# A fused attention and GLU layer: gate and up tiles in groups of their own, tanh and product read from the banks, ScalarE's order laid out by its own clock

## The chip, the cores and the metric

One core of one Trainium2 chip runs the whole layer in one launch. The metric is device time in microseconds (us), the median of several runs. A profiled execution of the kernel lies beside it.

Five engines work side by side, each with an instruction queue of its own, and wait for each other by semaphores: TensorE (PE in the profile; PEld are its weight loads), VectorE (DVE), ScalarE (ACT), GpSimd (POOL) and SyncE (SP), which issues most DMAs. Matmuls write into banks of the accumulator memory (PSUM), 128 partitions by 512 fp32 numbers each.

## What is computed

x has 2048 rows (tokens) of 1024 numbers. First comes attention with 32 query heads of width 32 that share one key and one value head, then a gated FFN of width 3584, each behind a layer norm and with a residual. Cut from the reference:

```
h  = x + A(layernorm(x));   h2 = h + B(layernorm(h))
A: q = x @ wq (32 heads); k = x @ wk; v = x @ wv
   p = softmax(q k^T / sqrt(32));  o = p v;  return o @ wo
B: g = x @ w_gate; u = x @ w_up
   return (sigmoid(g) * u) @ w_down
```

The sigmoid is taken as 0.5 * (1 + tanh(g/2)); the factor 0.5 is applied where the down product is added to the residual.

## The kernel before: tiles, stages and what sets the order

**Tiles.** The queries are cut into 8 chunks of 256 rows. For each chunk there are 8 head groups (four heads each, 128 numbers), and for each of these 8 score bursts: 512 bursts in all. One burst (s_burst, line 472) is 8 matmuls of two key tiles by four heads, written to two pairs of the six score banks S_ps. Each pair is turned into probabilities by one exponential on ScalarE (exps, line 494; 128x1024, so 1024 exponentials), which go to a ring of 18 tiles, Pr. The PV group of a head group (pv_group, lines 562 to 583) multiplies probabilities by V and sums them; from the tenth head group on, VectorE adds probabilities in pairs first (add_pair, lines 522 and 531), so that PE's sums of ones need fewer matmuls. Then come the output projection (wo_group), the second layer norm on VectorE and GpSimd, and a DMA transpose, which gives the chunk's FFN input in QT.

**FFN of a chunk before the change.** There are 28 tiles of 128 columns of w_gate and w_up, worked on in 14 pairs. A weight half is 256 columns (one pair) of one of the two matrices, 512 KB. gu_group (line 725 on) computes one tile: 8 matmuls of gate into columns 0 to 255 of a bank, 8 of up into columns 256 to 511 (line 734). VectorE copies the bank to a slot of gu (line 753), which frees it. After the second tile of a pair ScalarE takes the tanh in gu (line 761), and VectorE forms (1 + tanh) * up into hact (line 767). When the 14 pairs are done, four down groups of 28 matmuls follow (down_group, line 797), whose result VectorE adds to the residual (line 807).

**Banks.** Everything except the scores goes through two banks, X_ps. A group takes the one that comes free first (open_group) and holds it until its evacuation.

**Weights.** load_halves issues on SP the next half as soon as a slot is on the list half_free. During the first chunk there are four slots (wgu); parts of QT, of Pr and of kT join later, as they come out of use: 21 in the end. A half is given back after its last matmul, in the second tile of the pair. w_down is loaded once, in 14 pieces on GpSimd's queue (load_wd), which hang on score bursts 84 to 110.

**Order.** The order of every engine's instructions is laid out when the program is built. The Python code keeps a clock for each engine with assumed costs (T_EXP 0.91, T_TANH 0.53 and so on) and a time for each semaphore value (_Ctr.at). The main loop stands at PE's clock and picks what PE does next: a score burst as soon as the first exponential of the burst before it is due; else a PV group; else a projection, a gate/up or a down group, matmul by matmul, so that bursts cut into groups. A burst's two exponentials are put into ScalarE's queue at once (exps); before each, act_fill puts those tanhs whose input is due by then. VectorE's waiting work (pair sums, products, layer norms) lies on the list lo and is put into its queue by dve_fill when it is due, or by force when it is needed. The engines' queues run in this order, with semaphores for what must be waited for.

So PE runs scores, PV, projections and FFN of an earlier chunk interleaved until burst 511; behind it stands a tail of PE work without exponentials: the rest of the seventh chunk's FFN and that of the eighth.

Of the kernel before, what the change touches and what calls it, by code (L numbers as in the profile page):

```python
# [12 lines left out]
P = 128  # L13
# [4 lines left out]
class _Ctr:  # L18


    def __init__(self, sem, clk=None):
        self.sem = sem
        self.n = 0
        self.waited = {}
        self.clk = clk
        self.at = {}

    def inc(self, ins, cost=0.0, lat=0.0, k=1):
# [18 lines left out]
def when(*ticks):  # L47

    return max([0.0] + [t[0].at.get(t[1], 0.0) + 0.05 for t in ticks if t is not None])
# [25 lines left out]
def bass_sequential_preLN__grouped_kv_mqa__glu_gated_glu__prompt_kernel(  # L75
# [29 lines left out]
    RP = 18  # L105
# [9 lines left out]
    with ExitStack() as es:  # L115
# [94 lines left out]
        def _(unused):  # L210
# [172 lines left out]
            def k_group(p):  # L383
                c0 = 2 * p * P

                def evac(bank, tick):
                    act_fill(tick)
# [14 lines left out]
            def vq_group(p, qs):  # L402
# [11 lines left out]
                def evac(bank, tick):  # L414
                    act_fill(tick)
# [66 lines left out]
            def exps(k):  # L482
                for n in (2 * k, 2 * k + 1):
                    act_fill((c_s, n + 1))
                    need(act, (c_s, n + 1))
                    r = ring(k)
                    if r is None:
                        need(act, pv0_val.get(k // 2 - 3))
                    elif r >= RP // 2:
                        w = r - RP // 2 + 1  # L490
                        assert w <= pv_done[0], ("P ring", n, pv_done[0])
                        need(act, (c_pv, w), add_half.get(k - RP // 2))
                    pr = n % 3
                    c_e.inc(act.activation(out=p_tile(k, n % 2).rearrange("p (a b) -> p a b", a=2),  # L494
                                           in_=S_ps[:, 2 * pr:2 * pr + 2, :], func=ACTF.Exp, scale=SCALE), T_EXP, 0.12)

                if k // BPG >= G_SUM:
                    add_pair(k)
# [222 lines left out]
            gi = [0]  # L721
            gu_read = {}
            hact_val = {}

            def gu_group(c, ft):
                u = 2 * (c * NFP + ft // 2)
                f0 = (ft % 2) * P
                items = []
                for w in range(2):
                    for dt in range(DT):  # L730
                        def f(bank, w=w, dt=dt):
                            i = half_at[u + w]
                            need(pe, half_val[u + w])
                            ins = pe.matmul(bank[:, w * QC:(w + 1) * QC], lhsT=halves[i][:, dt, f0:f0 + P],  # L734
                                            rhs=QT[:, dt, c * QC:(c + 1) * QC], start=(dt == 0), stop=(dt == DT - 1))
                            tick = mm_done(ins, QC, dt == DT - 1)
                            if dt < DT - 1:
                                return None
                            if ft % 2 == 1:
                                half_free.append((i, [tick]))  # L740
                                if ft == NFT - 1 and w == 1 and c < NQC - 1:
# [3 lines left out]
                        items.append((QC * T_MM, f))  # L745

                def evac(bank, tick):
                    i1 = gi[0]
                    gi[0] += 1
                    r = i1 % NGU  # L750
                    force("s", lambda: i1 < NGU or i1 - NGU in gu_read)
                    need(dve, tick, gu_read.get(i1 - NGU))
                    v = c_dve.inc(dve.tensor_copy(out=gu[:, r, :], in_=bank), 0.61, 0.08)  # L753
                    if ft % 2 == 1:
                        g_ = gu[:, r - 1:r + 1, 0:QC]
                        u_ = gu[:, r - 1:r + 1, QC:2 * QC]
                        tv = [None]

                        def tanh():
                            need(act, v)  # L760
                            tv[0] = c_act.inc(act.activation(out=g_, in_=g_, func=ACTF.Tanh, scale=0.5), T_TANH, 0.1)  # L761

                        def stt():
                            while tv[0] is None:
                                act_work.popleft()[1]()
                            need(dve, tv[0], down_last[c - 1] if c else pv0_val[BPG - 1])
                            hact_val[(c, ft)] = c_dve.inc(dve.scalar_tensor_tensor(  # L767
                                out=hact[:, ft - 1:ft + 1, :], in0=g_, scalar=1.0, in1=u_, op0=ALU.add, op1=ALU.mult), 0.61, 0.08)
                            gu_read[i1 - 1] = gu_read[i1] = hact_val[(c, ft)]
                        act_work.append((v, tanh))  # L770
                        if k[0] >= NB:
                            act_work.popleft()[1]()
                        put("s", 0.61, stt, lambda: when(tv[0]) if tv[0] else None)
                    return v
                return _Group(items, evac, [hnT_val[c * TPQ], hnT_val[c * TPQ + 1]])
# [13 lines left out]
            def down_group(c, tt, dc):  # L789
                t = c * TPQ + tt  # L790
                items = []
                for ft in range(NFT):
                    def f(bank, ft=ft):
                        f1 = ft | 1
                        force("s", lambda: (c, f1) in hact_val)
# [29 lines left out]
            for c in range(NQC):  # L825
                ffn_list += [("gu", c, ft) for ft in range(NFT)]
# [21 lines left out]
            def next_group():  # L848
# [8 lines left out]
                if ffn_list:  # L857
# [4 lines left out]
                    c, u = a[1], 2 * (a[1] * NFP + a[2] // 2)  # L862
                    if c * TPQ + 1 in hnT_val and max(when(hnT_val[c * TPQ + i]) for i in range(TPQ)) <= now and u + 1 in half_val:
                        if when(half_val[u]) <= now + 0.3 and when(half_val[u + 1]) <= now + 1.0:
                            ffn_list.popleft()
                            return gu_group(c, a[2])
# [62 lines left out]
            while True:  # L929
                if q_done and not q_done[0].items and q_tick[0] is None:  # L930
                    q_tick[0] = (c_pe, c_pe.n)
                if q_tick[0] and wd_next[0] < NFP and k[0] >= WSL + WD_AT + 2 * wd_next[0]:
                    load_wd()
                kk = k[0]
                pv_ready = pv_next[0] < NQC * NQ and kk >= min(BPG * (pv_next[0] + 1) + 1, NB)
                can_s = kk < NB and pv_done[0] >= ring(kk) - RP // 2 + 1
                if can_s and k_pe[0] >= when((c_e, 2 * kk - 1)):
                    dve_fill(k_pe[0] + min([0.3] + [x.left() for x in (cur[0], pv[0]) if busy(x)]))
                    s_burst(kk)
                    exps(kk)  # L940
# [25 lines left out]
                starved = not q_list and bool(ffn_list) and ffn_list[0][0] == "gu" and ffn_list[0][1] * TPQ + 1 not in h_done  # L966
# [13 lines left out]
                if busy(cur[0]):  # L980
                    run_item(cur[0])
# [4 lines left out]
                if (pv_next[0] < NQC * NQ and kk > BPG * pv_next[0] + 1 and ffn_list and ffn_list[0][0] == "gu"  # L986
# [7 lines left out]
                if idle > 400 and act_work:  # L994
                    act_work.popleft()[1]()
                assert idle < 4000
            assert not lo
# [32 lines left out]
```

## Time and profile before

| | us |
|---|---|
| median of 3 runs | 1147.73 |
| lowest and highest | 1146.86 and 1151.37 |
| profiled execution | 1150.66 |
| its span (first to last instruction) | 1148.8 |
| PE busy / ScalarE busy / VectorE busy in the span | 1099.0 / 1012.9 / 860.0 |
| 1024 exponentials (line 494), busy | 949.0 and 15.6 |
| 112 tanhs (line 761), busy | 83.3 |
| 224 copies of banks (line 753), busy | 153.5 |
| 112 products (line 767), busy | 76.7 |

How to read it: the page's first part has each engine's busy time, the second the busy share in 40 slices of 28.7 us (9 is 90% or more). Groups are instructions of one line, with the mean of one in ns and the idle time of the engine before them. A ScalarE instruction's duration reaches over the start of the next one, so rates are read from starts, in the timeline. The chain of work goes back from the last instruction to what released it at each step; in order of time it reads as "start, duration, what". A table of windows has, for each stretch of time, the busy time of each engine and in brackets its instructions, then PE's granted clock, the DMA engines' share and their GB/s.

### The profile page before, as it was taken

The numbers are of one execution on the slowest core, as the hardware profiler recorded it, in microseconds if no ns is written. First come the engines' busy times: TensorE is split into PE (matmuls) and PEld (weight loads), VectorE is DVE, ScalarE is ACT, GpSimd is POOL, SyncE is SP. The second block draws the span as 40 slices with busy tenths as digits, with TensorE's granted clock in tenths as the row PEclk, the third lists the DMA queues.
The fourth block names the chain that finished last, engine by engine and source line by source line (L and its number), as shares of the span: only waits on it lengthen the run. The fifth ranks groups of instructions, "written<-read, shape, count | busy, mean of one in ns | idle before, by whom it ended". The sixth has DMA issues, their size and how long they took to land.

```text
span 1148.8 us, 33975 instructions
## 1 busy us (share of the span) xinstructions
PE 1099.0 (96%) x14875; PEld 667.7 (58%) x14944; DVE 860.0 (75%) x1540; ACT 1012.9 (88%) x1168; POOL 58.9 (5%) x122
## 2 busy tenths in 40 slices
PE   3799999889999999999999999999999999999998
PEld 2564446664457644775467644775467554766784
DVE  7433346877899878998889987999788987884351
ACT  5999999989999999999999999999999999970010
POOL 3200001100100001000100010001000000001000
PEclk9899999999999999999999999999999999999999
DMA  9910006964146612674146621764237551679800
GB/s 231 252 38 2 2 11 173 313 208 113 29 135 195 192 47 57 190 206 135 38 126 187 188 65 43 211 188 122 54 115 200 147 116 32 184 208 273 211 1 19
DMA packets 284180, 150.96 MB, mean 131 GB/s; under 512 B 40704, under 2 KB 278272, under 8 KB 284032
## 3 DMA queue, kind: packets, MB, share of 16 engines
q1 hardware_dynamic: 276256, 138.17, 45.9%
q0 software_dynamic: 2544, 9.44, 2.3%
q8 instruction: 117, 1.92, 0.7%
q10 hardware_dynamic: 5232, 1.18, 0.7%
q14 instruction: 31, 0.25, 0.1%
HBM read 136.18 MB, written 4.19 MB: 122 GB/s over the span
## 4 chain that ended last, share of the span: by engine, by line
PE 74%; ACT 11%; DVE 7%; issue 4%; DMA 3%; POOL 1%; DVEq 0%; ACTq 0%
PE X_ps L734 32%; PE X_ps L797 12%; PE S_ps L472 11%; ACT Pr L494 10%; PE X_ps L583 8%; PE X_ps L290 8%; DMA wgu<-in_B_w_up_dram 2%; PE X_ps L562 2%; DVE pairs L522 1%; PE X_ps L580 1%; DVE pairs L531 1%; DVE st L300 1%; ACT hact L494 1%; DVE st L678 1%; DMA zone<-hn 0%
## 5 line engine op out<-in xcount | busy, mean ns | idle before, releaser
L494 ACT ACTIVATE Pr<-S_ps 128x1024 bf16<-128x1024 f32 x1008 | 949.0, 1179 | 8.2 <-PE S_ps L472 8.1
L522 DVE TENSOR_TENSOR pairs<-Pr 128x1024 bf16<-128x1024 bf16 x432 | 290.6, 685 | 66.6 <-ACT Pr L494 61.8
L734 PE MATMUL X_ps<-QT,wgu 128*128 128x256 bf16 x2048 | 272.0, 275 | 5.9 <-DMA wgu<-in_B_w_up_dram 5.4
L734 PEld LDWEIGHTS X_ps<-QT,wgu 128*128 128x128 bf16 x2048 | 189.5, 98 | 63.9 <-issue 32.0
L797 PE MATMUL X_ps<-zone,hact 128*128 128x512 bf16 x852 | 205.6, 380 | 6.1 <-issue 4.8
L472 PE MATMUL S_ps<-QT,kT 32*128 32x256 bf16 x4096 | 204.3, 274 | 7.4 <-ACT Pr L494 4.2
L753 DVE COPY gu<-X_ps 128x512 f32<-128x512 f32 x224 | 153.5, 685 | 27.3 <-PE X_ps L734 25.2
L734 PE MATMUL X_ps<-QT 128*128 128x256 bf16 x1264 | 171.2, 273 | 0.0
L583 PE MATMUL X_ps<-Pr,V 128*32 128x256 bf16 x4032 | 162.4, 274 | 1.5 <-DVE gu L753 1.1
L761 ACT ACTIVATE gu<-gu 128x512 f32<-128x512 f32 x112 | 83.3, 744 | 85.8 <-DVE gu L753 85.8
L531 DVE TENSOR_TENSOR pairs<-pairs 128x1024 bf16<-128x1024 bf16 x216 | 148.7, 688 | 10.6
L472 PEld LDWEIGHTS S_ps<-QT,kT 32*128 32x128 bf16 x4096 | 60.8, 92 | 155.3 <-ACT Pr L494 136.2
L797 PEld LDWEIGHTS X_ps<-zone,hact 128*128 128x128 bf16 x896 | 78.6, 98 | 102.1 <-issue 22.5
L734 PEld LDWEIGHTS X_ps<-QT 128*128 128x128 bf16 x1264 | 116.8, 98 | 30.9 <-issue 18.2
L583 PEld LDWEIGHTS X_ps<-Pr,V 128*32 128x32 bf16 x4032 | 98.3, 96 | 27.8 <-issue 18.4
L290 PE MATMUL X_ps<-zone 128*128 128x256 bf16 (+2 forms) x501 | 77.2, 299 | 23.2 <-ACT hn L338 14.3
L767 DVE SCALAR_TENSOR_TENSOR hact<-gu 128x512 bf16<-128x512 f32 x112 | 76.7, 686 | 12.1 <-ACT gu L761 12.1
L601 DVE COPY ols<-X_ps 128x256 f32<-128x256 f32 x64 | 27.0, 422 | 69.0 <-PE X_ps L583 54.1
L290 PEld LDWEIGHTS X_ps<-zone 128*128 128x128 bf16 x512 | 39.4, 101 | 52.7 <-issue 14.7
L290 PE MATMUL X_ps<-wo,QT 128*128 128x512 bf16 x242 | 59.4, 380 | 1.6 <-issue 1.3
L307 POOL TENSOR_SCALAR vz<-mv 128x1 bf16<-128x1 bf16 (+1 forms) x24 | 9.1, 379 | 903.5 <-DVE mv L682 891.7
L807 DVE SCALAR_TENSOR_TENSOR hx<-X_ps,hx 128x512 bf16<-128x512 f32 x32 | 22.0, 688 | 41.9 <-PE X_ps L797 41.7
(54 smaller groups left out, 508.3 us busy)
## 6 DMA issues: line engine op xcount, KB each, us to landing
wgu<-in_B_w_gate_dram SPq DMA_DIRECT2D x72, 512.0 KB, 5.0
wgu<-in_B_w_up_dram SPq DMA_DIRECT2D x56, 512.0 KB, 5.1
QT<-in_B_w_up_dram SPq DMA_DIRECT2D x47, 512.0 KB, 5.2
QT<-in_B_w_gate_dram SPq DMA_DIRECT2D x32, 512.0 KB, 5.3
zone<-in_B_w_down_dram POOLq DMA_DIRECT2D x14, 512.0 KB, 7.0
hx<-in_A_x_dram SPq DMA_DIRECT2D x16, 256.0 KB, 2.9
out_dram<-hx SPq DMA_DIRECT2D x32, 128.0 KB, 1.7
Pr<-in_B_w_up_dram SPq DMA_DIRECT2D x8, 512.0 KB, 6.1
```

The costliest lines, as they stand in the source:

```text
L290: ins = pe.matmul(sel(bank), lhsT=a, rhs=b, start=(i == 0), stop=(i == last))
L472: ins = pe.matmul(S_ps[:, bank, kt * QC:(kt + 1) * QC], lhsT=kT4[DH * j:DH * (j + 1), (2 * b + kt) * P:(2 * b + kt + 1) * P], rhs=QT[DH * ...
L494: c_e.inc(act.activation(out=p_tile(k, n % 2).rearrange("p (a b) -> p a b", a=2), in_=S_ps[:, 2 * pr:2 * pr + 2, :], func=ACTF.Exp, scale= ...
L522: add_half[k] = slot_use[slot] = c_dve.inc(dve.tensor_tensor(out=pairs[:, slot, :].rearrange("p (j q) -> p j q", j=4), in0=p4[:, :, 0, :], ...
L531: slot_use[x] = slot_use[y] = c_dve.inc(dve.tensor_tensor(out=pairs[:, x, :], in0=pairs[:, x, :], in1=pairs[:, y, :], op=ALU.add), T_ADD, ...
L583: ins = pe.matmul(bank[DH * j:DH * (j + 1), 0:QC], lhsT=V[:, 2 * b + kt, :], rhs=rhs(j), start=first and summed, stop=last and not summed, ...
L601: dve.tensor_copy(out=ols[:, 0:QC], in_=bank[:, 0:QC])
L734: ins = pe.matmul(bank[:, w * QC:(w + 1) * QC], lhsT=halves[i][:, dt, f0:f0 + P], rhs=QT[:, dt, c * QC:(c + 1) * QC], start=(dt == 0), sto ...
L753: v = c_dve.inc(dve.tensor_copy(out=gu[:, r, :], in_=bank), 0.61, 0.08)
L761: tv[0] = c_act.inc(act.activation(out=g_, in_=g_, func=ACTF.Tanh, scale=0.5), T_TANH, 0.1)
L767: hact_val[(c, ft)] = c_dve.inc(dve.scalar_tensor_tensor(out=hact[:, ft - 1:ft + 1, :], in0=g_, scalar=1.0, in1=u_, op0=ALU.add, op1=ALU.m ...
L797: ins = pe.matmul(bank, lhsT=hact[:, ft, tt * P:(tt + 1) * P], rhs=wd[:, ft, dc * 512:(dc + 1) * 512], start=(ft == 0), stop=(ft == NFT - 1))
```

## The change

1. A group now computes both tiles of a pair for one matrix: a gate group (16 matmuls, one half) and an up group (16 matmuls, the other half) take the place of two mixed groups. A half is given back after its own group.
2. The copies are gone. ScalarE takes the tanh from the gate group's bank into a slot of gu (half as wide as before, so four pairs fit), and this frees the bank. VectorE forms the product from gu and the up group's bank, which frees that one.
3. Exponentials are no longer queued at once. A burst puts its two on exp_queue; tanhs wait on act_work with the time from which they can start; act_next picks, by ScalarE's clock, what can start first (a tanh up to 0.1 us later than an exponential goes ahead). act_run does so up to PE's clock at each step of the main loop, exp_emit when something needs an exponential that is not queued yet; exp_guess estimates its time until then.
4. open_group asks a bank that waits for a tanh for an estimated time (free). If none is free yet, the main loop lets up to 3 us pass on PE's clock, so that something else may come between.
5. A gate or an up group is picked when its own half is due within 0.3 us; before, a group asked for its gate half within 0.3 and its up half within 1.0.

The core of the diff:

```diff
@@ class _Ctr, need
+    def time(self, n):
+        if self.guess is not None and n > self.n:
+            return self.guess(n)
+        return self.at.get(n, 0.0)
...
+    for t in ticks:
+        if t is not None and t[0].emit is not None and t[1] > t[0].n:
+            t[0].emit(t[1])
@@ open_group
+            def bank_time(b):
+                f = bank_free[b]
+                return 1e9 if f == "open" else f(False) if callable(f) else when(f)
...
-                b = min((when(bank_free[b]), b) for b in range(2) if bank_free[b] != "open")[1]
+                b = min((bank_time(b), b) for b in range(2) if bank_free[b] != "open")[1]
                 g.bank = b
-                need(pe, bank_free[g.bank])
-                bank_free[g.bank] = "open"
+                f = bank_free[b]
+                need(pe, f(True) if callable(f) else f)
+                bank_free[b] = "open"
@@ ScalarE's order
-            def act_fill(*ticks):
-                while act_work and when(act_work[0][0]) < max(k_act[0], when(*ticks)) + 0.1:
+            def act_next():
+                s_e = max(k_act[0], exp_ready(exp_queue[0])) if exp_queue else 1e9
+                s_t = max(k_act[0], act_work[0][2]()) if act_work else 1e9
+                return (s_t, False) if s_t <= s_e + 0.1 else (s_e, True)
+            def act_one(is_exp):
+                if is_exp:
+                    one_exp(exp_queue.popleft())
+                else:
                     act_work.popleft()[1]()
+            def act_run(until):
+                while exp_queue or act_work:
+                    s, is_exp = act_next()
+                    if s > until:
+                        return
+                    act_one(is_exp)
+            def exp_emit(n):
+                while c_e.n < n:
+                    act_one(act_next()[1])
+            def exp_guess(n):
+                t = k_act[0]
+                for x in range(c_e.n, n):
+                    t = max(t, exp_ready(x)) + T_EXP
+                return t + 0.12
@@ the groups
-            def gu_group(c, ft):
...
-                    v = c_dve.inc(dve.tensor_copy(out=gu[:, r, :], in_=bank), 0.61, 0.08)
...
+            def half_group(c, fp, w, evac, after):
+                u = 2 * (c * NFP + fp) + w
+                items = []
+                for j in range(2):
                     for dt in range(DT):
...
+                            need(pe, half_val[u])
+                            ins = pe.matmul(bank[:, j * QC:(j + 1) * QC], lhsT=halves[i][:, dt, j * P:(j + 1) * P],
                                             rhs=QT[:, dt, c * QC:(c + 1) * QC], start=(dt == 0), stop=(dt == DT - 1))
...
+                            if j == 1 and dt == DT - 1:
                                 half_free.append((i, [tick]))
...
+            def gate_group(c, fp):
...
+                    def tanh():
+                        need(act, tick, gu_read.get(n - NGU))
+                        tanh_val[n] = c_act.inc(act.activation(out=slot, in_=bank, func=ACTF.Tanh, scale=0.5), T_TANH, 0.1)
...
+                    act_work.append((tick, tanh, lambda: when(tick, gu_read.get(n - NGU))))
+                    return free
...
+            def up_group(c, fp):
...
+                    while n not in tanh_val:
+                        act_one(act_next()[1])
+                    need(dve, tick, tanh_val[n], down_last[c - 1] if c else pv0_val[BPG - 1])
+                    hact_val[(c, 2 * fp + 1)] = gu_read[n] = c_dve.inc(dve.scalar_tensor_tensor(
+                        out=hact[:, 2 * fp:2 * fp + 2, :], in0=slot.rearrange("p (a b) -> p a b", a=2), scalar=1.0,
+                        in1=bank.rearrange("p (a b) -> p a b", a=2), op0=ALU.add, op1=ALU.mult), 0.61, 0.08)
@@ next_group, main loop
-                    if c * TPQ + 1 in hnT_val and max(when(hnT_val[c * TPQ + i]) for i in range(TPQ)) <= now and u + 1 in half_val:
-                        if when(half_val[u]) <= now + 0.3 and when(half_val[u + 1]) <= now + 1.0:
+                    if c * TPQ + 1 in hnT_val and max(when(hnT_val[c * TPQ + i]) for i in range(TPQ)) <= now and u in half_val:
+                        if when(half_val[u]) <= now + 0.3:
...
+                act_run(k_pe[0])
...
-                    exps(kk)
+                    exps(kk, now=False)
...
+                    if cur[0].bank is None and k_pe[0] + 0.02 < min(bank_time(b) for b in range(2)) < k_pe[0] + 3.0:
+                        k_pe[0] += 0.02
+                        dve_fill(k_pe[0])
+                        continue
```

More of the change, by code (lines that the diff above doesn't have):

```diff
@@ L26, in __init__ @@
         self.at = {}
+        self.guess = self.emit = None
     def inc(self, ins, cost=0.0, lat=0.0, k=1):
@@ L480, in _, with one_exp, exps @@
             pv0_val = {}
[L482 to L497, printed above, removed]
+            def one_exp(n):
+                k = n // 2
+                need(act, (c_s, n + 1))
+                r = ring(k)
+                if r is None:
+                    need(act, pv0_val.get(k // 2 - 3))
+                elif r >= RP // 2:
+                    w = r - RP // 2 + 1
+                    assert w <= pv_done[0], ("P ring", n, pv_done[0])
+                    old = k - RP // 2
+                    if old >= G_SUM * BPG:
+                        force("p", lambda: old in add_half)
+                    need(act, (c_pv, w), add_half.get(old))
+                pr = n % 3
+                c_e.inc(act.activation(out=p_tile(k, n % 2).rearrange("p (a b) -> p a b", a=2),
+                                       in_=S_ps[:, 2 * pr:2 * pr + 2, :], func=ACTF.Exp, scale=SCALE), T_EXP, 0.12)
+            def exps(k, halves=(0, 1), now=True):
+                exp_queue.extend(2 * k + i for i in halves)
+                if now:
+                    exp_emit(2 * k + halves[-1] + 1)
+                if k // BPG >= G_SUM and 1 in halves:
                     add_pair(k)
@@ L754, in evac @@
[L754 to L773, printed above, removed]
```

63 lines of the change are left out of this document (31 added, 32 removed).

## The prediction, made before the changed kernel ran

> **What bounds the kernel now.** I read the page's first three parts first.
>
> ```profile
> PE 1099.0 (96%) x14875; PEld 667.7 (58%) x14944; DVE 860.0 (75%) x1540; ACT 1012.9 (88%) x1168; POOL 58.9 (5%) x122
> ...
> ACT  5999999989999999999999999999999999970010
> ...
> DMA  9910006964146612674146621764237551679800
> ```
>
> TensorE (PE) is busy nearly all the time, and ScalarE (ACT) too, until the last exponential (about 1024 us, slice 36); only then is ScalarE free. VectorE (DVE), which the change relieves, has a quarter of the span to spare. So I ask per stage whether PE or ScalarE ends last. For that I need the price of each piece of PE work. The chain of work in order of time has them:
>
> ```profile
> 344.41 0.33 PE S_ps L472 x8
> 344.74 1.53 PE X_ps L734 x13
> ...
> 1072.99 48.91 PE X_ps L734 x448
> 1121.95 10.74 PE X_ps L797 x49
> ```
>
> In the tail 448 gate/up matmuls follow each other at 48.91/448 = 0.109 us, down matmuls at 0.219. Thirteen between two score bursts take 1.53 = 13 x 0.109 + 0.11: a change between scores, attention sums (PV) and full-array matmuls costs 0.11 us. A score burst of 8 takes 0.33, so 0.22 and one such change. Four PV matmuls of one step take 0.11. ScalarE's prices come from the timeline:
>
> ```profile
> 341.11 7.49 ACT L494 ACTIVATE Pr<-S_ps 128x1024 bf16<-128x1024 f32 x8
> ...
> 348.46 0.65 ACT L761 ACTIVATE gu<-gu 128x512 f32<-128x512 f32 x1
> 348.98 3.79 ACT L494 ACTIVATE Pr<-S_ps 128x1024 bf16<-128x1024 f32 x4
> ```
>
> Eight exponentials start over 7.35 us, and the next one starts 0.52 us after a tanh: instructions overlap by their ends, so what counts is start to start: 0.905 to 0.92 for an exponential (0.904 is the commonest), 0.52 for a tanh. A burst feeds two exponentials, 1.81 us.
>
> Now I lay both program orders side by side, eight score bursts at a time, price each engine's work by these rows and take the larger. Bursts are counted from 0 to 511; times are where the burst stands in the trace.
>
> | bursts | larger of PE and ACT, before | measured before | larger, after |
> |---|---|---|---|
> | 80 to 120 (176.8 to 265.1 us) | 79.2 | 88.3 | 80.5 |
> | 120 to 160 (to 340.1) | 74.3 | 75.0 | 73.9 |
> | 160 to 511 (to 1022.4) | 682.9 | 682.3 | 683.4 |
>
> From 340 us on, the larger of the two explains the trace to 0.1%. PE alone would need 680.5 of the 682.9: the two engines are balanced to a few tenths per cent, so relief for one alone buys almost nothing. Only bursts 80 to 120 hold real waiting, 9.1 us. The windows and the chain tell what it is:
>
> ```profile
> 205.00:210.00 5.00, 4.78 (x53) 3.41 (x51) 4.90 (x9) 4.71 (x6) 0.72 (x1) 1.00 1.10 322
> ...
> 240.00:245.00 5.00, 2.16 (x18) 1.36 (x19) 2.02 (x5) 3.09 (x5) 0.72 (x1) 0.86 1.10 320
> ```
>
> ```profile
> 201.56 6.41 DMA wgu<-in_B_w_up_dram
> ...
> 219.35 8.21 DMA wgu<-in_B_w_up_dram
> ...
> 234.13 8.66 DMA wgu<-in_B_w_up_dram
> ```
>
> The last column is GB/s, the one before it the busy share of the 16 DMA engines: saturated at about 320. There the weight halves of the first FFN chunk and w_down come in together, only four half slots exist, and PE stands up to 3 us waiting for an up half.
>
> **The change, part by part.**
>
> *VectorE.* 224 copies of 685 ns go: 153 us off VectorE. The 112 products stay; one operand now comes from a bank. Line 767 (operands in SBUF) takes 686 ns, line 807 (one operand a bank) 688, so nothing is added. VectorE's 75% lay beside PE and ScalarE, which are full: I put the gain at nothing. Nine waits of PE's PV steps for VectorE (2.1 us in all, by the spacing of PE's weight loads) bound it from above; nothing of this relief can lose.
>
> *Tanh from the bank.* No row shows a tanh that reads a bank. The nearest: four copies of 256 columns from SBUF (line 876) start 0.306 us apart; the exponential after a 256-column copy from a bank (line 389) starts after 0.264. So 0.042 less is one bound (0.478) and 0.52 the other; I take the middle, 0.50, since function and output type differ from both rows. Over the 92 tanhs among bursts 80 to 511 that is 1.8 us of ScalarE (0 to 3.9), but in the stretches with tanhs PE has 16.3 us of work per eight bursts against ScalarE's 16.0, so PE covers it: the table moves by 0.5 between the two bounds.
>
> *PE's order.* The matmuls are the same 14944. Changes between kinds fall from 1124 to 1118, 0.7 us, already in the table. But the split moves. After the last burst stood 595 gate/up matmuls, now 628: 33 x 0.109 = 3.6 us more in the tail, where nothing runs beside them. The reason shows in bursts 120 to 160: PE has 65.1 us of work there against 71.6 before, while ScalarE needs 73.9: the first chunk's FFN is used up earlier, PE runs dry, and the work missing there is paid at the end.
>
> *Banks.* A gate bank is now freed by ScalarE, behind exponentials. Of 112 tanhs, 70 stand in ScalarE's order one exponential short of all bursts issued at the gate group's end, 36 after all, 6 two short. PE's next user of that bank comes at least 1.75 us (an up group of 16) later in all but five cases. A score burst in between waits for the very exponential that the tanh follows, which ties the two queues together: priced by rows, the tanh is done 0.22 us or more before PE needs it, save twice (PV groups, 0.6 and 0.7 us). Cost: 1.3 us; none in bursts where PE's order has the slack anyway. An up bank waits for a tanh long done and 0.69 of product, less than the 1.75 of the next group. Behind a waiting product on VectorE stand the pair sums, which PV needs; with 153 us freed I cost that at nothing, and if a product waited as line 767 does now (12.1 us over 18) it would still be VectorE's idle time.
>
> *Weight halves.* This is the one gain. Before, both halves of a pair are held for 24 of its 32 matmuls; now each for 16. So the time from giving a slot back to needing it again, two pairs later, grows by 8 matmuls: about 0.9 us, with a share of the bursts 1.0. Where pairs follow closely (4.07 us), it goes from 5.1 to 6.1 us; halves take 5.5 to 8.9 us to land in this stretch. SP issues the same DMAs in nearly the same order, POOL's w_down loads hang on the same bursts. Six large waits shrink by up to 1 us each, those behind them with them. Bounds: nothing, or all 9.1. Against all of it stands bandwidth: three pairs per 16.3 us and w_down's four 0.52 MB loads are 5.2 MB, 322 GB/s, just what the windows show at best. I take 6.5 off, 2.6 us of waits left. The Trainium skill (DMA: Bandwidth & Descriptors, Specifications) gives a core about 358 GB/s from HBM; no window here passes 322. By its figure the lack would be one of latency alone, and an estimate would put all 9.1 us back, 1144.6 instead of 1147.2; rival 3 holds that case.
>
> **Sum.** +1.3 (80 to 120) - 0.4 - 0.0 + 0.5 (160 to 511) + 3.6 (tail) + 1.3 (banks) - 6.5 (halves) - 0.3 (waits for VectorE) = -0.5 us. The profiled execution took 1150.66 (span 1148.8), 2.9 above the median 1147.73 of runs from 1146.86 to 1151.37; the difference is taken off the median: **1147.2 us**, no change.
>
> **Rivals.**
> 1. *The halves give nothing* (bandwidth alone binds: the engines are at 1.1 of their share in most of the stretch). Then the tail's 3.6 and the rest stay: 1147.2 + 6.5 = 1153.7. Against: 230 to 235 us moves only 130 GB/s, so slots, not bandwidth, bound part.
> 2. *ScalarE stands at a tanh* (the slower side). A tanh now waits for PE itself, and exponentials wait behind it. By the two orders, priced by rows, ScalarE comes to a tanh 0.3 us or more after the gate group's end. It decides where PE runs over 0.3 us later against ScalarE than laid out. For it: DMA waits of 0.5 to 3 us strike PE inside groups. Against: the same bursts hold both engines together, and after 260 us the spacing of PE's weight loads shows one wait over 0.6 us. If the 92 tanhs lost 0.12 us each on average, 11 us: 1158. The Trainium skill (PSUM — Partial Sum Buffer, Engine vs sequencer instructions) calls ScalarE's queue strictly first in, first out, which is this rival's ground; here line 761 idled 85.8 us in 19 waits, nearly all after the last exponential, so its price among bursts is not shown.
> 3. *Faster*: all 9.1 us of waits go, the tanh takes 0.478 and VectorE's 2.1 us of waits vanish: 1147.2 - 2.6 - 0.5 - 1.8 = 1142.3; with the bank waits absent 1141.
> 4. *The order does not do what it says* (the planner's clock is off, so tanhs are late and banks with them): 1.3 becomes some 5, 1151.
>
> **Chances.** Forecast (1144.5 to 1150) 0.49, rival 1 0.16, rival 2 0.12, rival 3 0.15, rival 4 0.08. Half a per cent, 5.7 us, is about what a measurement of this kernel can tell: faster is below 1142.0, slower above 1153.5. Of rival 3 two thirds lie below; half of rival 1 lies above, and rival 2 whole: faster 0.10, same 0.70, slower 0.20. The range, 1141.5 to 1154, leaves out rival 2 (0.12), the upper end of rival 1 (0.05) and the lower of rival 3 (0.03).
>
> **What would show it.** Line 753 gone; tanh start to start near 0.48 to 0.52; bursts 160 to 511 again about 682 us; the stretch from burst 80 to 120 near 83 instead of 88 us with shorter DMA pieces in its chain; last exponential about 4 us earlier, and a tail 3.6 longer. I am wrong if PE waits for line 801 (tanh) by several us in total, if ScalarE's idle time before tanhs grows among the bursts, or if exponentials themselves change pace.

## The result, and the profile after

The changed kernel took 1155.29 us (median of 5 runs, 1151.48 to 1156.39), the kernel before 1148.18 in the runs beside it (1146.86 to 1151.37): a ratio of 1.0053, 95% interval 1.0034 to 1.0072. It is slower by half a per cent, where 1147.2 in 1141.5 to 1154 was forecast. The profiled execution took 1155.29, its span 1153.5, 4.7 more than the span before. That execution of before was itself 2.5 above its median, so the medians lie further apart than the spans. PE's granted clock goes with this: of the 53 runs of before beside the experiments, the twelve with a mean granted clock of 0.997 or more took 1144.83 to 1148.51 us, the eight with 0.993 or less 1149.99 to 1152.5, and the profiled execution had 0.992.

The page of the changed kernel, first and second part:

```profile
PE 1098.6 (95%) x14874; PEld 668.4 (58%) x14944; DVE 733.3 (64%) x1316; ACT 1012.3 (88%) x1168; POOL 58.5 (5%) x122
...
ACT  5999999999999999999999999999999999960110
PEclk9999999999979999999999999999999999999999
DMA  9910006992047621665146630764236550689700
```

VectorE lost 127 us of work (153 was forecast), and nothing came of it, as forecast. New is the 7 in PE's granted clock in slice 11 (317 to 346 us). Lines 472, 494, 734, 761, 797 of before are 516, 540, 782, 801, 846 here, line 583 is 633. ScalarE's timeline:

```profile
345.61 3.82 ACT L540 ACTIVATE Pr<-S_ps 128x1024 bf16<-128x1024 f32 x4
349.23 0.69 ACT L801 ACTIVATE gu<-X_ps 128x512 f32<-128x512 f32 x1
349.71 3.88 ACT L540 ACTIVATE Pr<-S_ps 128x1024 bf16<-128x1024 f32 x4
```

From the tanh's start to the next exponential's it is 0.48 us; the commonest distance of all is 0.477, the lower bound of the forecast. The chain of work in order of time, in the tail:

```profile
1021.22 0.33 PE S_ps L516 x8
1021.55 2.07 PE X_ps L782 x18
...
1037.74 15.72 PE X_ps L782 x144
1053.51 10.74 PE X_ps L846 x49
```

Prices of matmuls have not moved (15.72/144 = 0.109). But between the last output projection and the seventh chunk's down groups 144 gate/up matmuls follow each other; before there were 112 in 12.23 us. The difference is the 3.5 us by which the tail grew (32 of the 33 matmuls more that the prediction counted).

Measured as in the prediction, by where bursts stand (us). The stretches are those of the one profiled execution, whose own time stands beside the median. PE work is what the order of the program holds, by the same prices. The tail goes from burst 511 to the last weight load. Half clock is the time between 170 and 350 us in which PE's granted clock was 0.5:

| kernel | median of runs | profiled execution | bursts 80-120 | PE work there | 120-160 | PE work there | 160-511 | tail | half clock |
|---|---|---|---|---|---|---|---|---|---|
| before | 1148.18 | 1150.66 | 88.3 | 76.8 | 75.0 | 71.6 | 682.3 | 123.1 | 6.8 |
| changed | 1155.29 | 1155.29 | 86.8 | 79.7 | 77.2 | 65.1 | 682.7 | 126.6 | 13.6 |
| e1_late_pick | 1143.94 | 1144.15 | 82.7 | 77.1 | 74.8 | 72.7 | 682.1 | 122.7 | 0 |
| e2_exp_at_once | 1150.25 | 1153.72 | 88.8 | 79.3 | 76.5 | 69.7 | 682.4 | 122.7 | 10.2 |
| e3_gate_copied | 1155.11 | 1157.31 | 89.5 | 79.8 | 77.0 | 64.9 | 683.1 | 125.0 | 13.6 |
| e4_pe_kept_warm | 1151.94 | 1151.96 | 86.0 | 79.7 | 74.3 | 70.5 | 682.7 | 126.6 | 0 |
| e5_late_giveback | 1155.19 | 1155.80 | 87.9 | 79.7 | 76.4 | 65.1 | 682.7 | 126.6 | 10.2 |
| e6_before_late_pick | 1143.46 | 1143.46 | 80.9 | 72.6 | 75.3 | 74.9 | 683.3 | 121.2 | 0 |
| e7_half_wdown | 1148.69 | 1148.22 | 80.7 | 79.7 | 76.0 | 65.1 | 682.7 | 126.6 | 10.2 |
| e8_later_pick | 1142.51 | 1142.51 | 79.7 | 74.0 | 75.4 | 75.0 | 682.7 | 122.7 | 0 |
| e9_old_rules | 1140.94 | 1139.51 | 81.8 | 75.5 | 76.0 | 75.9 | 682.9 | 118.0 | 0 |
| e10_before_new_pick | 1154.03 | 1152.88 | 87.1 | 78.9 | 75.6 | 68.8 | 682.8 | 124.8 | 6.8 |

In before the 6.8 us at half clock lie in bursts 80 to 120 (178.8 to 182.2 and 243.6 to 247.0 us), in e2 and e3 3.4 of theirs (from 196 us); all others lie in bursts 120 to 160. e2's execution was 3.5 and e3's 2.2 above their medians, the slowest of their runs, so their stretches are on the long side.

From before to changed: -1.5 + 2.2 + 0.4 + 3.5 = 4.6, the 4.7 of the spans. The first two places are these. In the first stretch PE still blocks on weight halves, now at the start of gate groups (chain of work in order of time, changed kernel):

```profile
185.93 7.88 DMA wgu<-in_B_w_gate_dram
...
203.97 7.30 DMA wgu<-in_B_w_gate_dram
...
221.33 8.02 DMA wgu<-in_B_w_gate_dram
...
239.40 7.78 DMA wgu<-in_B_w_gate_dram
```

These are PE's waits for halves, of before and of the changed kernel (in all, times, longest), and the windows of bursts 80 to 120, of before and of the changed kernel (after the stretch and its length: PE, PEld, DVE, ACT, POOL busy with instructions, granted clock, DMA share, GB/s):

```profile
PE X_ps L734 <- DMA wgu<-in_B_w_up_dram: 5.4, 5, 2.9
PE X_ps L782 <- DMA wgu<-in_B_w_gate_dram: 4.8, 4, 1.5
```

```profile
176.80:265.10 88.30, 81.37 (x1105) 55.09 (x1106) 71.16 (x125) 80.69 (x94) 10.18 (x14) 0.96 0.83 241
176.80:263.60 86.80, 80.70 (x1119) 54.96 (x1120) 57.25 (x98) 81.35 (x95) 10.19 (x14) 1.00 0.89 257
```

With one wait of 0.3 us for an up half the changed kernel's waits come to 5.1 us in five, so in sum they hardly moved; they went from up halves to gate halves. What did change is the clock: 0.96 in before, for two stretches of 3.4 us at half clock, in which PE was busy throughout. At half the speed that is up to 3.4 us lost in before, and nothing in the changed kernel.

In the second stretch PE runs dry. The windows of the changed kernel, then of before:

```profile
315.00:320.00 5.00, 1.88 (x28) 0.39 (x20) 3.53 (x6) 5.00 (x6) 0.00 (x0) 0.59 0.07 23
320.00:325.00 5.00, 4.65 (x80) 2.59 (x84) 3.63 (x8) 3.76 (x5) 0.00 (x0) 0.50 0.30 57
```

```profile
315.00:320.00 5.00, 4.09 (x38) 1.36 (x36) 4.23 (x10) 5.00 (x6) 0.56 (x2) 1.00 0.40 78
320.00:325.00 5.00, 4.09 (x58) 2.50 (x59) 4.84 (x8) 5.00 (x7) 0.00 (x0) 1.00 0.24 80
```

PE is busy 1.88 of 5 us, its clock goes to one half, and in the next window ScalarE, full until then, idles 1.24 us. The timeline of the changed kernel shows how (PE, then ScalarE):

```profile
320.35 0.61 PE L516 MATMUL S_ps<-QT,kT 32*128 32x256 bf16 x8 [1.22 <-ACT Pr L540]
...
321.15 2.35 PE L633 MATMUL X_ps<-Pr,V 128*32 128x256 bf16 x40
...
323.64 0.61 PE L516 MATMUL S_ps<-QT,kT 32*128 32x256 bf16 x8
...
324.29 1.94 ACT L540 ACTIVATE Pr<-S_ps 128x1024 bf16<-128x1024 f32 x2 [1.24 <-PE S_ps L516]
```

At half clock 40 PV matmuls take 2.35 us (at full clock 40 took 1.27), the score burst behind them is late, and ScalarE waits for it. Over bursts 120 to 160 its exponentials, where they follow each other, lie 2.9 us in all further apart than 0.905 each, against 0.7 before.

### The profile page after: what moved, and what is told of

The parts are those of the page before. It is cut to its first block, busy times and chain, and to the rows that moved or that the text cites. A ratio compares the mean times of both kernels' runs of the same rounds, so it can differ in the third digit from the quotient of the medians.

```text
span 1153.5 us, 33948 instructions
## 1 busy us (share of the span) xinstructions
PE 1098.6 (95%) x14874; PEld 668.4 (58%) x14944; DVE 733.3 (64%) x1316; ACT 1012.3 (88%) x1168; POOL 58.5 (5%) x122
## 4 chain that ended last, share of the span: by engine, by line
PE 71%; ACT 14%; DVE 6%; issue 4%; DMA 3%; POOL 1%; DVEq 0%; ACTq 0%; another core or an unknown queue 0%
PE X_ps L782 31%; PE X_ps L846 13%; ACT Pr L540 12%; PE S_ps L516 11%; PE X_ps L633 8%; PE X_ps L304 6%; DMA wgu<-in_B_w_gate_dram 3%; PE X_ps L612 2%; DVE pairs L572 2%; PE X_ps L630 1%; DVE st L314 1%; DVE pairs L581 1%; ACT hact L540 1%; DVE st L728 1%; ACT gu L801 1%
## 5 line engine op out<-in xcount | busy, mean ns | idle before, releaser
L572 DVE TENSOR_TENSOR pairs<-Pr 128x1024 bf16<-128x1024 bf16 x432 | 294.4, 687 | 166.4 <-ACT Pr L540 158.3
L782 PE MATMUL X_ps<-QT,wgu 128*128 128x256 bf16 x2048 | 261.8, 274 | 5.1 <-DMA wgu<-in_B_w_gate_dram 4.8
L782 PE MATMUL X_ps<-QT 128*128 128x256 bf16 x1248 | 160.5, 273 | 0.0
L801 ACT ACTIVATE gu<-X_ps 128x512 f32<-128x512 f32 x112 | 75.8, 677 | 88.6 <-PE X_ps L782 87.7
L821 DVE SCALAR_TENSOR_TENSOR hact<-gu,X_ps 128x512 bf16<-128x512 f32 x112 | 76.3, 682 | 67.8 <-PE X_ps L782 67.1
L304 PE MATMUL X_ps<-zone 128*128 128x256 bf16 (+2 forms) x501 | 77.2, 299 | 23.4 <-ACT hn L352 14.2
L651 DVE COPY ols<-X_ps 128x256 f32<-128x256 f32 x64 | 26.9, 421 | 65.1 <-PE X_ps L633 54.2
L612 PE MATMUL X_ps<-pairs,ones 128*32 128x256 bf16 x864 | 53.5, 276 | 0.8 <-DVE pairs L581 0.7
```

Of the source, the lines that this page charges most:

```text
L304: ins = pe.matmul(sel(bank), lhsT=a, rhs=b, start=(i == 0), stop=(i == last))
L572: add_half[k] = slot_use[slot] = c_dve.inc(dve.tensor_tensor(out=pairs[:, slot, :].rearrange("p (j q) -> p j q", j=4), in0=p4[:, :, 0, :], ...
L612: ins = pe.matmul(bank[DH * j:DH * (j + 1), QC:2 * QC], lhsT=ones[:], rhs=pairs[:, HOME[b], j * QC:(j + 1) * QC], start=False, stop=b == S ...
L651: dve.tensor_copy(out=ols[:, 0:QC], in_=bank[:, 0:QC])
L782: ins = pe.matmul(bank[:, j * QC:(j + 1) * QC], lhsT=halves[i][:, dt, j * P:(j + 1) * P], rhs=QT[:, dt, c * QC:(c + 1) * QC], start=(dt == ...
L801: tanh_val[n] = c_act.inc(act.activation(out=slot, in_=bank, func=ACTF.Tanh, scale=0.5), T_TANH, 0.1)
```

## The experiments

**Theory A**, formed from this: no engine got slower. The planner starts the first chunk's pairs earlier than the halves come. So PE still blocks on halves with score bursts queued behind the blocked group; the chunk's work is used up earlier; PE runs dry in bursts 144 to 160, at half clock besides; and what could have filled it is paid in the tail. **Theory B**: bandwidth alone sets the first stretch. **Theory C**: tanh from the bank, and ScalarE's queue, cost the time. A theory D comes in with e6 alone.

**e1_late_pick** (changed kernel):

```diff
-                        if when(half_val[u]) <= now + 0.3:
+                        if when(half_val[u]) <= now + (0.3 if c else -2.0):
```

> The changed kernel, but in the first chunk a gate or up group is picked only when its half was due 2 us ago by the planner's clock (instead of 0.3 us ahead). Theory A (the planner spent the earlier refills on starting pairs earlier, so PE still blocks on weight halves in bursts 80 to 120, runs dry in bursts 144 to 160, and pays the deferred work in the tail): the larger of PE and ScalarE is 79.7 us in bursts 80 to 120, measured 80 to 83 instead of 86.8; bursts 120 to 160 take 75 instead of 77.2, no half clock at 316 us; the tail is 122 instead of 126.6 because 587 instead of 628 gate/up matmuls are left. About 1144 us, 8 to 12 below the changed kernel, at or below the kernel before. Theory B (bandwidth alone sets bursts 80 to 120): that stretch stays at 86 to 88 and only the tail's 4 us and the clock's 2 us come back, 1149. Theory C (ScalarE's queue stands at tanhs whose input comes from PE): no stage but the tail moves, 1151.

1143.94 us, ratio to before 0.996 (0.9944 to 0.9976). Every stretch went where A had put it: 82.7, 74.8, 682.1, 122.7, and no half clock. B fails as the whole story, and C.

**e2_exp_at_once** (changed kernel):

```diff
-                    exps(kk, now=False)
+                    exps(kk)
```

> The changed kernel with one part undone: a burst's two exponentials go to ScalarE's queue at once, as in the kernel before; groups, tanh and product stay. Theory A: what counts is where PE's work falls. In this order 588 gate/up matmuls are left for the tail and bursts 120 to 160 hold 69.7 us of PE work (65.1 in the changed kernel, 71.6 before), so tail 122 and those bursts 75 to 76; bursts 80 to 120 as in the changed kernel, 84 to 87. About 1148 us. Theory C: ScalarE's order by its own clock is what makes the tanh from the bank bearable; without it the waits for tanh grow in every stretch with tanhs and bursts 160 to 511 take 690 us or more instead of 682.7, 1158 or more.

1150.25, ratio 1.0018 (1.0003 to 1.0033). Tail 122.7 and 682.4 as A had it; bursts 120 to 160 took 76.5, with half clock, a little over the 75 to 76 expected; bursts 80 to 120 took 88.8 where 84 to 87 was expected, in an execution 3.5 above the median that had the half clock there too. C fails: ScalarE's new order is not what makes the tanh bearable.

**e3_gate_copied** (changed kernel, gate_group's evacuation):

```diff
+                    need(dve, tick, gu_read.get(n - NGU))
+                    v = c_dve.inc(dve.tensor_copy(out=slot, in_=bank), 0.61, 0.08)
                     def tanh():
-                        need(act, tick, gu_read.get(n - NGU))
-                        tanh_val[n] = c_act.inc(act.activation(out=slot, in_=bank, func=ACTF.Tanh, scale=0.5), T_TANH, 0.1)
+                        need(act, v)
+                        tanh_val[n] = c_act.inc(act.activation(out=slot, in_=slot, func=ACTF.Tanh, scale=0.5), T_TANH, 0.1)
...
+                    act_work.append((v, tanh, lambda: when(v)))
+                    return v
```

> The changed kernel, but VectorE copies the gate group's bank to gu (112 copies) and frees it, and the tanh is taken in gu; groups and ScalarE's order by its own clock stay. Theory A: the tanh from the bank costs and gains nothing; bursts 160 to 511 take 682 to 684, bursts 80 to 160 stay near 164, the tail is 1.7 shorter by its 614 matmuls left: 1152 to 1155 us. Theory C: ScalarE and the gate bank were the loss, 3 us or more come back among bursts 160 to 511 and 80 to 160, 1149 or less.

1155.11, ratio 1.005 (1.0034 to 1.0066): the same as the changed kernel. Bursts 160 to 511 and the tail came as A had it (683.1 and 125.0); bursts 80 to 160 took 166.5 instead of 164, in the slowest execution of the eight. Taking the tanh out of the bank gives nothing back; C falls.

**e4_pe_kept_warm** (changed kernel; warm() is called where the main loop lets PE's clock pass, and picks a free bank b):

```diff
+                if not 140 <= k[0] <= 164 or not b:
+                    return
...
+                pe.matmul(X_ps[:, b[0], 0:256], lhsT=wo[:, 0, 0:P], rhs=wo[:, 0, 0:256], start=True, stop=True)
```

> The changed kernel, with some 50 matmuls that belong to nothing (128x256, into a free bank, read by nobody) where PE would idle in bursts 140 to 164; everything else is in the same order. Theory A with the clock as its part: PE's granted clock stays at 1.0 from 310 to 335 us, bursts 120 to 160 take 74 to 74.5 instead of 77.2, everything after is earlier by as much: 2.5 us below the changed kernel. If the half clock is only seen there and costs nothing (ScalarE ends last anyway), bursts 120 to 160 stay at 77 or grow by the added work, 0 to +2 us.

1151.94, ratio 1.0031 (1.0016 to 1.0046), against 1.0053 (1.0034 to 1.0072) for the changed kernel. The intervals overlap, so what the clock cost is read from the stretch: bursts 120 to 160 took 74.3 as expected. Its windows:

```profile
315.00:320.00 5.00, 3.74 (x46) 2.02 (x47) 3.59 (x6) 5.00 (x7) 0.00 (x0) 1.00 0.01 3
320.00:325.00 5.00, 4.47 (x100) 2.51 (x100) 3.80 (x9) 5.00 (x6) 0.00 (x0) 1.00 0.31 59
```

The trace has 39 useless matmuls; with them PE's clock stays at 1.00 and ScalarE at 5.00 of 5, in the changed kernel's order of work: the half clock cost 2.9 us of the stretch. The kernels with the same order bear this out: with 0, 10.2, 10.2 and 13.6 us at half clock (e4, e7, e5, changed) the stretch takes 74.3, 76.0, 76.4 and 77.2. In the changed kernel no gap of PE between 312 us and the fall at 315.9 was longer than 0.91 us, nor any later one there longer than 1.44, and PE was busy 1.8 of the 3.4 us before the fall. The Trainium skill (TensorE: Matmul & The Clock Gate, What's actually happening) lists the half clock as the state after an idle window of about 3.4 us. The Trainium skill (TensorE: Matmul & The Clock Gate, Why this matters for your kernels) asks for no idle gaps of PE over about 3 us. Here the clock fell without any gap of that length, and the measurement decides.

**e5_late_giveback** (changed kernel, half_group; the up group gives the gate half back after its eighth matmul, and a gate group gives nothing back):

```diff
+                            if w == 1 and j == 0 and dt == DT - 1:
+                                half_free.append((half_at[u - 1], [tick]))
+                                load_halves()
+                            if w == 0:
+                                return tick
```

> The changed kernel, but a gate half is given back 8 matmuls later, after the first half of the up group, as in the kernel before; no engine's order moves (three late groups only read other slots). It measures the term that the prediction put at 6.5 us by itself. If the earlier refill is worth what was predicted (about 1 us at each of some six waits), bursts 80 to 120 go from 86.8 to 91 to 93 and the time rises by 4 to 6 us, 1159 to 1161. Theory A's other part (the waits are set by when PE asks, which lies too early by the planner's clock, and by the bandwidth both loads share): 0 to 2 us, 1155 to 1157.

1155.19, ratio 1.0063 (1.0043 to 1.0082), against 1.0053. Bursts 80 to 120: 87.9 for 86.8. PE waits for halves 5.4 us, in six waits, for 5.1. The earlier refill of the gate halves, on which PE now waits, is worth about 1 us in that stretch, and nothing that the medians show. Its chain tells why:

```profile
187.48 6.56 DMA wgu<-in_B_w_gate_dram
...
205.50 6.96 DMA wgu<-in_B_w_gate_dram
...
223.83 6.90 DMA wgu<-in_B_w_gate_dram
...
242.08 6.42 DMA wgu<-in_B_w_gate_dram
```

Asked for later, the halves take 0.3 to 1.4 us less: they wait for the DMA engines wherever they are asked. e5 speaks of the gate halves alone: the up halves, which a pair now needs 8 matmuls later than before, keep their gain in it, and no run takes that back by itself.

**e6_before_late_pick** (the kernel before, nothing of the change):

```diff
-                        if when(half_val[u]) <= now + 0.3 and when(half_val[u + 1]) <= now + 1.0:
+                        if when(half_val[u]) <= now + (0.3 if c else -0.5) and when(half_val[u + 1]) <= now + (1.0 if c else 0.2):
```

> The kernel before with nothing of the change, but in its first chunk a group is picked only when its gate half was due 0.5 us ago and its up half is due within 0.2 us (before: due within 0.3 and 1.0). Theory A: the late pick, not the groups, is what the better version lives on. PE and ScalarE give 78.4, 75.1 and 683.3 for bursts 80 to 120, 120 to 160, 160 to 511, and 582 instead of 595 gate/up matmuls are left for a tail of 121.5; with 3 to 4 us of waits left in the first stretch that is about 1143 us. Theory D (the late pick helps only with gate and up groups of their own, since only these refill early): bursts 80 to 120 stay at 86 to 88, 1148.

1143.46, ratio 0.9956 (0.9933 to 0.998); bursts 80 to 120 took 80.9. The late pick serves the kernel before as well; D fails.

**e7_half_wdown** (changed kernel; half of w_down is left out of the computation):

```diff
-                wd_val[0] = dma(pool, wd[:, f0:f0 + 2, :],
+                wd_val[0] = dma(pool, wd[:, f0:f0 + 1, :],
...
-                                        rhs=wd[:, ft, dc * 512:(dc + 1) * 512], start=(ft == 0), stop=(ft == NFT - 1))
+                                        rhs=wd[:, ft & ~1, dc * 512:(dc + 1) * 512], start=(ft == 0), stop=(ft == NFT - 1))
```

> The changed kernel, but each of the 14 w_down loads brings only its first half, 0.26 MB, and the down matmuls read that half twice: half of w_down is left out of the computation. No engine's order moves. Theory B (in the first chunk the halves wait for bandwidth that w_down's loads take): bursts 80 to 120 fall from 86.8 to 81 to 82 and the time by 5, 1150; bursts 120 to 160 stay at 77 and the tail at 126.6, since PE's order is the same. If the waits are the refill's own time only, with bandwidth to spare: 85 to 87, 1154 to 1155.

1148.69, ratio 1.0004 (0.9987 to 1.0021): 6.6 below the changed kernel. Bursts 80 to 120 fall to 80.7 with PE's order unchanged, and no wait of PE for a half is left; the other stretches move by 1.2 or less. So B is right about where the waits come from: w_down's loads. With e8 it is half of the truth: there the same bytes leave no wait either, since PE asks late.

**e8_later_pick**: as e1, with -3.0 in place of -2.0.

> As e1_late_pick, but a half must have been due 3 us ago instead of 2. The same 587 gate/up matmuls are left for the tail. Theory A: PE asks later still, so the 3 us of waits that e1_late_pick kept in bursts 80 to 120 (82.7 against 79.7) shrink to 1 or 2, the larger of PE and ScalarE there is 78.9, bursts 120 to 160 75.2 and the rest 683.8: 1142 to 1144 us. If the margin only trades waits for PE idling elsewhere, no difference from 1143.9.

1142.51, ratio 0.9956 (0.994 to 0.9972). Bursts 80 to 120 took 79.7, less even than expected, though PE has only 74.0 us of work there. No wait of PE for a DMA is left: PE idles between groups and no longer inside them, score bursts go ahead, and ScalarE is busy for all of the 79.7 us. One 5 us window moved 335 GB/s, for 322 at most before. The Trainium skill (DMA: Bandwidth & Descriptors, Specifications) gives a core about 358 GB/s from HBM. No window here reaches that.

**e9_old_rules** (changed kernel; e5's edit, and):

```diff
-                        if when(half_val[u]) <= now + 0.3:
+                        if when(half_val[u]) <= now + 0.3 and (a[0] == "u" or u + 1 in half_val and when(half_val[u + 1]) <= now + 1.0):
```

> The changed kernel with the two old rules on weight halves together: the gate half is given back 8 matmuls later (as in e5_late_giveback), and a gate group is picked only when its up half is in the queue and due within 1.0 us. Groups of one matrix, tanh and product from the banks and ScalarE's order by its own clock all stay. Here PE's order does move: 75.5 us of PE work in bursts 80 to 120, 75.9 in 120 to 160 (65.1 in the changed kernel), 551 gate/up matmuls left for the tail. Theory A: the loss comes from the planner's two rules on halves alone, not from anything that an engine does. Larger of both 79.4 plus 1 to 2 us of waits, 75.9, 683.6, tail 118: about 1140 us, the best of all. Theory C (tanh and banks cost ScalarE or PE time): some of it remains, 1147 or more.

1140.94, ratio 0.9939 (0.9917 to 0.9961), the fastest version, with all else of the change in place. Its bursts 80 to 120 stand at 175.6 to 257.4 us and 120 to 160 at 257.4 to 333.4. Two windows that cover most of them:

```profile
176.80:256.00 79.20, 74.68 (x1075) 51.62 (x1068) 55.79 (x96) 77.56 (x91) 10.21 (x14) 1.00 0.90 261
256.00:332.00 76.00, 75.96 (x1006) 39.37 (x1005) 59.14 (x106) 76.00 (x86) 4.06 (x8) 1.00 0.34 90
```

PE is busy 75.96 of 76 us where it ran dry in the changed kernel. Each rule alone leaves PE's order as in the changed kernel: e5 has the give-back alone, and with the pick alone the code lays out the very program of the changed kernel. Only both together spread the first chunk.

**e10_before_new_pick** (the kernel before):

```diff
-                        if when(half_val[u]) <= now + 0.3 and when(half_val[u + 1]) <= now + 1.0:
+                        if when(half_val[u]) <= now + 0.3 and when(half_val[u + 1]) <= now + 3.0:
```

> The kernel before with one condition changed towards the change: a group is picked when its up half is due within 3.0 us instead of 1.0. Nothing else, mixed groups and copies stay. PE's order becomes like the changed kernel's: 78.9 us of PE work in bursts 80 to 120 (76.8 before), 68.8 in 120 to 160 (71.6), 615 instead of 595 gate/up matmuls in the tail. Theory A: slower than before by the same path: bursts 80 to 120 at 87 to 90, 120 to 160 at 75 to 77, tail 124.8; 1150 to 1153 us. Theory C: without the new groups nothing is lost, 1148.

1154.03, ratio 1.0052 (1.0029 to 1.0075), 1 us more than A expected: one number in the planner brings as large a loss to the kernel before, without a group, a tanh or a queue of the change. The stretches show only part of it, since this execution was 1.2 below its median and that of before 2.3 above the median of before here: bursts 80 to 120 took 1.2 less, bursts 120 to 160 0.6 more and the tail 1.7 more. The chain has the wait for a half, the windows the half clock:

```profile
237.75 8.69 DMA wgu<-in_B_w_up_dram
```

```profile
315.00:320.00 5.00, 1.94 (x37) 0.66 (x36) 4.76 (x8) 5.00 (x7) 0.31 (x1) 0.97 0.08 26
320.00:325.00 5.00, 3.91 (x68) 2.08 (x72) 3.81 (x8) 3.97 (x6) 0.00 (x0) 0.50 0.47 110
```

## Why the prediction was wrong

- **"Weight halves. This is the one gain ... I take 6.5 off": the step that failed.** The term was mis-sized, and in part it priced something else. PE's waits for halves were 5.4 us in five waits before and 5.1 in five after; the earlier refill of the gate halves is worth about 1 us (e5). The prediction took all 9.1 us by which bursts 80 to 120 exceeded the larger of both engines for such waits, though its own row for 240 to 245 us has a granted clock of 0.86; up to 3.4 us of them were the half clock. So the 2.8 us by which the stretch came closer to its work (it fell by 1.5, where its work grew by 1.3) need no gain of the refill: the clock that did not fall there can give them all.
- **Why it failed.** The step counted the longer time from give-back to need as time for the transfer. But the order was already another one: pairs were asked for earlier (79.7 for 76.8 us of PE work in the stretch), and the DMA engines, shared with w_down, were full (e7). The planner's clock gives a half 2.3 us and 2.0 of delay and leaves w_down's queue out; in the trace halves take up to 8 us. The signs named for this term failed too: the chain's DMA pieces take 7.3 to 8.0 us, not less than before, and the last exponential starts 1.1 us later instead of 4 earlier.
- **Rival 1** (the halves give nothing, 1153.7, at 0.16) came nearest. Its reason, bandwidth alone, is half of the truth (e1, e8), and it has no half clock, so that its number came so near is in part luck.
- **Bursts 120 to 160, "-0.4": wrong, +2.2.** The prediction saw PE run dry there and priced it by the larger of two engines at full clock. PE, busy 1.8 of 3.4 us, lost its clock, and the late score bursts stopped ScalarE. With the clock kept the stretch is 2.9 us shorter (e4).
- **The tail, "+3.6": right**, 3.5. The reason given (the first chunk is used up earlier) is right too: with the chunk spread, e1, e8 and e9 leave 587, 587 and 551 gate/up matmuls, and their tails are 122.7, 122.7 and 118.0.
- **Bursts 160 to 511, "+0.5": right**, +0.4. They take 682.1 to 683.3 in all twelve kernels.
- **Tanh from the bank:** 0.477, the lower end of 0.478 to 0.52, and covered by PE as said. **VectorE:** 127 us of relief and no gain, as said. **Banks, "1.3 us":** PE's two PV steps that wait for a tanh stand at 514.9 and 934.0 us with 0.8 and 0.9, where 0.6 and 0.7 was forecast.
- **Rival 2** (ScalarE stands at a tanh): not seen; e2 and e3 take away its parts and bursts 160 to 511 do not move.
- The sum was -0.5. With a gain of 1.0 for the 6.5 and 2.2 for the -0.4 it is +7.6, against +7.1 by medians and +4.6 by the stretches of the profiled executions. The stretches of before hold its half clock, up to 3.4 us, which the sum leaves out; an estimate with it is +4.2 or more. How much of the 3.4 us reached the end is not shown, and the first stretch varies by about 2 us between executions of the same order (86.0 to 87.9 in changed, e4 and e5).

What stays open is whether groups of one matrix with tanh and product in the banks are worth anything by themselves. With the planner's rules mended they reach 1140.94, the kernel before with its rule mended 1143.46; the intervals (0.9917 to 0.9961 and 0.9933 to 0.998) overlap.

## What to carry to other kernels

Where two engines are balanced, a stretch of an in-order queue is priced by the larger of both, and that held to 0.1% for 682 us, closer than prices rounded to a few thousandths of a us can promise; what moves the time is where waits stand. An engine that idles before it takes up a group costs little, while the same wait inside the group holds everything queued behind it: a planner should ask late for what a DMA brings, and count every queue that shares the DMA engines. When a change alters the rule by which work is picked, look first at the order that comes out, where work runs dry and what is left for the end, and only then at the instructions.

## What the runs showed of the hardware

- PE's granted clock fell to one half at 311 to 322 us in six of the kernels, each time where PE was busy for 0.9 to 1.8 of the 3.4 us before, while its longest gap was 0.9 to 1.44 us. In the kernel before it fell at 178.8 us after 3.4 us with 1.9 busy and no gap over 0.52. Other stretches of 3.4 us with 1.5 busy (e10, up to 248.0 us) or 1.8 (e4, up to 211.7 us) had no fall, so no limit by this share is shown. In the seven kernels with a fall the half clock lasted 6.8 to 13.6 us in all between 170 and 350 us, and PV matmuls took 1.85 times as long (2.35 for 1.27 us).
- A tanh of 512 columns from a bank keeps ScalarE 0.477 us, from SBUF 0.520, start to start; for copies of 256 columns these are 0.264 and 0.306 us, much the same difference (0.043 and 0.042).
- A product with one operand in a bank took 682 ns, with both in SBUF 686.
- Of the 5 us windows from 180 to 260 us the fullest moved 321 to 337 GB/s, whatever the order of the requests; 311 in e7, whose w_down loads are half as large.
